# Windowed attention and gated MLP on one core: all engines' order as one explicit list, scores of a pair in one burst, norms by single tiles

## The chip, the core and the metric

The kernel runs on one core of one Trainium2 chip. The core has a matrix engine (TensorE; its matmuls are PE in the profile, its weight loads PEld), a vector engine (VectorE, DVE), an activation engine (ScalarE, ACT), a general engine (GpSimd, POOL) and a queue that issues the transfers from and to memory (SyncE, SP). Each engine works through its own list of instructions in order and waits on semaphores that the others raise. The on-chip memory SBUF holds operands; TensorE writes into PSUM, from where VectorE and ScalarE read.

The metric is the device time of one execution in microseconds (us). The profile adds where that time goes. Its span runs from the first to the last instruction and is a little shorter than the device time.

## What is computed

Eight batches, eight heads, 576 positions, head size 64. Attention looks back over a window of 128 positions, with a bias that falls linearly with the distance. Its output x (576 x 512 per batch) goes through a gated MLP with a spatial mixing matrix and is added to the result.

```python
scores = scale * np.matmul(q, k.transpose(0, 1, 3, 2))
bias = slopes[:, None, None] * (-np.abs(rel).astype(np.float32))[None, :, :]
mask = (rel >= 0) & (rel < window)
scores = np.where(mask, scores + bias[None], -1000000000.0)
attn = np.exp(scores - np.max(scores, axis=-1, keepdims=True))
attn = attn / (np.sum(attn, axis=-1, keepdims=True) + 1e-09)
x = np.matmul(attn, v)                       # heads side by side: (B, S, 512)
h = gelu_tanh(x @ w_in)                      # 512 -> 1024
u, v = h[..., :512], h[..., 512:]
v_n = (v - mean(v)) / np.sqrt(var(v) + 1e-06) * g_ln
v_s = np.einsum('ts,bsd->btd', w_sg, v_n) + b_sg[None, :, None]
out = x + (u * v_s) @ w_out
```

## The kernel before

The attention is worked off in 32 *pairs* (two heads of one batch; pair n belongs to batch n // 4), the MLP in 8 *blocks*, one per batch, each after the four pairs of its batch. Everything is fp32; MLP products are made from a high and a low part of each operand (hi·hi, hi·lo, lo·hi), so an MLP product is three matmuls, all written as one source line each (L466 to L468, L489 to L491, L551 to L553).

A pair's steps (class `Pair`; the letters are the names that order tables use) are:

- q, L: loads of q/k and of v (SP).
- a, c (`scores`, L320): scores of the first and of the second half of the queries, 64 x 64 corners of the array, four at work at once; they go into tiles of the PSUM pool ps_s.
- A, C (`minima`, L260): on VectorE, the bias is added, the sign turned, and each row's minimum kept in stats. n (`copy_minima`) copies the minima into nb.
- E or e, f (`exps`, L363): exponentials with row sums on ScalarE.
- R (inverse, VectorE), r, s, S (scaling by GpSimd, L378).
- t, T, z (transposes on TensorE into the PSUM pool ps_a, L388 and L401), X, Y (`masked`, VectorE: two mask products per head into px), P (ScalarE copy).
- v (`values`, L421 and L418): px times v on TensorE into ps_a; x (`gather`, ScalarE) into xf.
- h, l, k (`high`, `low`, `low_tail`): xf is cut into a high and a low part, xs. h and k run on ScalarE for the first five pairs and as casts on VectorE for the rest (L260); l runs on GpSimd (L438).

A block (`mlp_block`) has the parts v (sums L489 to L491, then gelu and `norm` per 128 rows), t (`v_tail`, the last 64 rows, L517, L519, and their norm into vA and vB), u (four sums L466 to L468 with a gelu over all), y (four gating sums with ws, L551 to L555, a product on VectorE, and its high and low part) and o (four output sums, the addition of x, and the transfer out). The gating sums need all norms: their twelve first matmuls read vn, the last two vA and vB. `norm` takes statistics on VectorE, a power on GpSimd, the centring on VectorE, the high part on ScalarE (L479) and the low part on VectorE (L482). A v part does gelu over two 512-wide tiles at once into one buffer vg.

Weights come as 64-bit values; twelve chunks of them are decoded (`split64`) by two ScalarE steps, three VectorE steps (L235, L237, L239), and three more on GpSimd and ScalarE.

What sets the order: the first five pairs, the decoding of w_in and some v sums of batch 0 stand in a table START, whose steps are chained on each engine. Afterwards a loop emits pair stages and block parts by small tables (PLAN), the decoding of w_sg and w_out rides along with one step for every second VectorE instruction (class `Vec`), and the tile framework's own scheduler places the instructions on the engines by its reckoning of time. TensorE's order can thus break a run of scores with a matmul of a block.

Of the kernel before, what the change touches and what calls it, by code (L numbers as in the profile page):

```python
# [21 lines left out]
def attention_gmlp(  # L22
# [116 lines left out]

    NS = 2 * (T + 1)  # L140
# [18 lines left out]
    def stage(src, cast=F32):  # L159

        w = mlp.tile([P, src.shape[1]], src.dtype, name="wst", tag="g", bufs=NF)
        nc.sync.dma_start(w[0:src.shape[0]], src)
        return w

    def w_chunk(k):

        half, c = 1 - k // NC, k % NC
        hs = slice(half * F, (half + 1) * F)
        return w_in[c * P:(c + 1) * P, hs], lambda w: split64(wi[:, 0, c, hs], wi[:, 1, c, hs], w, scratch[:, k, :])

    def chunks():

        for c in range(T):
            yield w_sgT[c * P:(c + 1) * P, :], lambda w, c=c: split_sg(c, w)
        yield w_sgT[T * P:S, :], split_sg_tail
        for c in range(NF):
            yield w_out[c * P:(c + 1) * P, :], lambda w, c=c: grouped(split64(wo[:, 0, c, :], wo[:, 1, c, :], w, att.tile([P, F], F32, name="tmp", tag="e", bufs=4)), (3, 1, 2, 1))

    def grouped(steps, sizes):
        for n in sizes:  # L180
            for _ in range(n):
                next(steps, None)
            yield

    def decode():

        jobs = chunks()
        staged = []
        def ahead(n):
            while len(staged) < n:  # L190
                job = next(jobs, None)
                if job is None:
                    return
                staged.append((stage(job[0]), job[1]))
        ahead(NEARLY)
        while staged:
            w, steps = staged.pop(0)
            yield from steps(w)
            ahead(NEARLY)

    def split_sg(c, st):
        split(ws[:, 0, c, :], ws[:, 1, c, :], st)
        yield

    def split_sg_tail(st):
        nc.sync.dma_start(st[R:2 * R], w_sgT[T * P:S, :])
        nc.scalar.activation(wsA, st, AF.Copy)
        nc.gpsimd.tensor_tensor(wsB[0:R], st[0:R], wsA[0:R].bitcast(F32), ALU.subtract)
        yield

        sb = mlp.tile([P, S], F32, name="wst", tag="g", bufs=NF)
        sh = mlp.tile([P, S], F32R, name="wsh", tag="g", bufs=NF)
        sel = const.tile([P, 1], F32, name="bsel")
        nc.vector.memset(sel[R:R + 2], -1.0)
        nc.vector.memset(sel[R:R + 1], 0.0)
        for r in range(2):
            nc.sync.dma_start(sb[R + r:R + r + 1, :], b_sg.rearrange("(o t) -> o t", o=1))
        nc.scalar.activation(sh[R:R + 2], sb[R:R + 2], AF.Copy)
        nc.vector.scalar_tensor_tensor(out=wsB[R:R + 2], in0=sh[R:R + 2].bitcast(F32), scalar=sel[R:R + 2], in1=sb[R:R + 2], op0=ALU.mult, op1=ALU.add)
        nc.vector.memset(vB[R:R + 2].bitcast(F32), 1.0)  # L220
        yield
# [26 lines left out]

    def split(hi, lo, x):
        nc.scalar.activation(hi, x, AF.Copy)  # L250
        nc.gpsimd.tensor_tensor(lo, x, hi.bitcast(F32), ALU.subtract)  # L251

    class Vec:

        credit = 0.0
        done = 0

        def __getattr__(self, name):
            def call(*args, **kw):
                inst = getattr(nc.vector, name)(*args, **kw)  # L260
                if self.steps is not None:
                    self.credit += RATE
                    while self.credit >= 1.0:
                        self.credit -= 1.0
                        self.done += 1
                        with tc.issue_after(inst.ins):
                            next(self.steps, None)
                return inst
            return call

    vec = Vec()
    vec.steps = None
# [12 lines left out]
    class Pair:  # L285
# [25 lines left out]
        def scores(self, t2):  # L311
            qk, heads = self.qk, self.heads
            W = 3 * R
            if t2 == 0:
                self.pr = [att.tile([P, T, P], F32, name="e", bufs=4) for _ in range(2)]
                self.e0 = att.tile([R, 2 * R], F32, name="e0", bufs=2)
            banks = self.banks[t2] = [ps_s.tile([P, 512], F32, name="ps_s") for _ in range(2)]
# [17 lines left out]
            burst(insts)  # L335

        def shift(self, h, dst, src, bs, acc):

            vec.tensor_tensor_reduce(out=dst, in0=src, in1=bs, scale=-1.0 / math.sqrt(D), scalar=3e38, op0=ALU.add, op1=ALU.min, accum_out=acc)

        def minima(self, t2):
            W = 3 * R
            banks, pr, nm = self.banks.pop(t2), self.pr, self.nm
            for j in range(2):
                h = 2 * self.hp + j
                sv = banks[j][:, 0:2 * W].rearrange("p (t b c) -> p t b c", t=2, b=3)
# [7 lines left out]
        def copy_minima(self):  # L354

            nb = att.tile([P, NS], F32, name="nb", bufs=3)
            vec.tensor_copy(nb, self.nm)
            self.nm = nb
# [325 lines left out]
```

## Time and profile before

| what | us |
|---|---|
| device time, median of 3 runs | 675.34 |
| lowest, highest | 674.81, 679.94 |
| the profiled execution's own time | 675.89 |
| its span | 674.2 |
| PE busy / DVE / ACT / POOL | 638.0 / 417.2 / 334.1 / 244.2 |

Mean granted TensorE clock 0.983. Rows of the profile name the line, engine and operation, then output tile <- input tiles with their shapes, then a count; in timeline rows the first two numbers are start and length in us, and the bracket at the end tells how long the engine stood idle before it and what ended that. A score or a value matmul leaves two records; MLP matmuls and transposes leave one. A matmul's row is as long as the matmul takes from entering to leaving the array, and the next one starts before it ends: what TensorE can do per us is read from start to start. A run, here, is an unbroken sequence of TensorE records of one kind.

### The profile page before, as it was taken

The numbers are of one execution on the slowest core, as the hardware profiler recorded it, in microseconds if no ns is written. First come the engines' busy times: TensorE is split into PE (matmuls) and PEld (weight loads), VectorE is DVE, ScalarE is ACT, GpSimd is POOL, SyncE is SP. The second block draws the span as 40 slices with busy tenths as digits, with TensorE's granted clock in tenths as the row PEclk, the third lists the DMA queues.
The fourth block names the chain that finished last, engine by engine and source line by source line (L and its number), as shares of the span: only waits on it lengthen the run. The fifth ranks groups of instructions, "written<-read, shape, count | busy, mean of one in ns | idle before, by whom it ended". The sixth has DMA issues, their size and how long they took to land.

```text
span 674.2 us, 14921 instructions
## 1 busy us (share of the span) xinstructions
PE 638.0 (95%) x5664; PEld 562.6 (83%) x5664; DVE 417.2 (62%) x1372; ACT 334.1 (50%) x979; POOL 244.2 (36%) x241
## 2 busy tenths in 40 slices
PE   3788796999999999999999999999999999999997
PEld 2666585887898889888899889889799888999997
DVE  5887996556646665655576656646576657553511
ACT  7676776434574326633645336742645345731420
POOL 1786657332134322551324321453226321360120
PEclk9998797999999999999999999999999999999999
DMA  8648330233212312224122322133221331001001
GB/s 273 209 128 241 114 125 8 74 106 111 72 48 80 112 53 73 73 74 143 57 59 69 107 73 73 41 103 116 69 59 56 108 106 36 1 2 71 0 1 71
DMA packets 55931, 57.24 MB, mean 85 GB/s; under 512 B 8498, under 2 KB 45362, under 8 KB 55860
## 3 DMA queue, kind: packets, MB, share of 16 engines
q1 hardware_dynamic: 55860, 56.28, 26.7%
q8 instruction: 45, 0.74, 0.5%
q14 instruction: 26, 0.21, 0.1%
HBM read 46.83 MB, written 9.44 MB: 83 GB/s over the span
## 4 chain that ended last, share of the span: by engine, by line
PE 75%; DVE 13%; ACT 7%; DMA 2%; issue 2%; POOL 1%; ACTq 0%; DVEq 0%; POOLq 0%
PE ps_m L466 9%; PE ps_m L467 8%; PE ps_m L468 8%; PE ps_s L320 7%; PE ps_a L418 7%; PE ps_m L551 5%; PE ps_m L552 5%; PE ps_m L553 5%; PE ps_a L388 4%; PE ps_m L489 3%; PE ps_m L490 3%; PE ps_m L491 3%; ACT e L363 3%; DVE vn L482 2%; DVE px L260 2%; DVE st L474 2%
## 5 line engine op out<-in xcount | busy, mean ns | idle before, releaser
L378 POOL TENSOR_TENSOR e<-e,rr 128x512 f32<-128x512 f32 (+1 forms) x96 | 77.9, 833 | 170.7 <-DVE rr L260 140.9
L363 ACT ACTIVATE e<-e,nb 128x128 f32<-128x128 f32 x270 | 101.7, 378 | 28.8 <-DVE nb L260 28.7
L320 PE MATMUL ps_s<-qk 64*64 64x192 f32 (+2 forms) x1280 | 79.7, 326 | 12.3 <-DMA qk<-qkT 8.0
L466 PE MATMUL ps_m<-xs,wi 128*128 128x288 f32 x256 | 79.2, 309 | 0.9 <-ACT vg L509 0.5
L551 PE MATMUL ps_m<-ws,vn 128*128 128x288 f32 x256 | 79.1, 309 | 0.0
L466 PE MATMUL ps_m<-g,wo 128*128 128x288 f32 x256 | 77.9, 305 | 0.2 <-DVE xf L564 0.2
L477 POOL TENSOR_TENSOR rs<-rs,mhalf 128x1 f32<-128x1 f32 (+1 forms) x40 | 35.3, 893 | 116.2 <-DVE rs L476 116.2
L552 PE MATMUL ps_m<-ws,vn 128*128 128x288 f32 x256 | 77.1, 301 | 0.0
L468 PE MATMUL ps_m<-xs,wi 128*128 128x288 f32 x256 | 76.9, 300 | 0.0
L553 PE MATMUL ps_m<-ws,vn 128*128 128x288 f32 x256 | 76.8, 300 | 0.0
L467 PE MATMUL ps_m<-g,wo 128*128 128x288 f32 x256 | 76.7, 301 | 0.0
L467 PE MATMUL ps_m<-xs,wi 128*128 128x288 f32 x256 | 76.6, 299 | 0.0
L320 PEld LDWEIGHTS ps_s<-qk 64*64 64x64 f32 x1280 | 50.2, 141 | 31.0 <-issue 18.9
L468 PE MATMUL ps_m<-g,wo 128*128 128x288 f32 x256 | 75.7, 297 | 0.0
L251 POOL TENSOR_TENSOR g<-u,g 128x576 fp32r<-128x576 f32 x32 | 45.4, 1419 | 68.3 <-ACT g L250 62.8
L418 PE MATMUL ps_a<-px,vt 128*64 128x128 f32 (+1 forms) x1152 | 64.4, 267 | 4.6 <-issue 2.8
L418 PEld LDWEIGHTS ps_a<-px,vt 128*64 128x64 f32 x1152 | 59.3, 142 | 10.3 <-issue 8.9
L260 DVE CUSTOM_DVE_ANT_0 e<-ps_s,bias 128x128 f32<-128x128 f32 (+1 forms) x256 | 57.1, 265 | 0.4
L260 DVE TENSOR_TENSOR px<-ps_a,m_old 128x512 f32<-128x512 f32 x64 | 43.8, 685 | 19.8 <-PE ps_a L388 19.5
L489 PE MATMUL ps_m<-wi,xs 128*128 128x512 f32 x128 | 52.5, 410 | 2.4 <-ACT xs L433 2.4
L438 POOL TENSOR_TENSOR xs<-xf,xs 128x576 fp32r<-128x576 f32 x32 | 46.4, 1461 | 21.1 <-DVE xs L260 20.9
L551 PEld LDWEIGHTS ps_m<-ws,vn 128*128 128x128 f32 x256 | 49.2, 192 | 3.7 <-issue 2.2
(113 smaller groups left out, 1487.6 us busy)
## 6 DMA issues: line engine op xcount, KB each, us to landing
qk<-qkT SPq DMA_DIRECT2D x32, 576.0 KB, 3.9
vt<-v_in SPq DMA_DIRECT2D x64, 256.0 KB, 3.2
outT<-xf SPq DMA_DIRECT2D x32, 288.0 KB, 2.1
wst<-w_in SPq DMA_DIRECT2D x8, 512.0 KB, 7.2
vt<-v_in SPq DMA_DIRECT2D x64, 32.0 KB, 2.9
wst<-w_out SPq DMA_DIRECT2D x4, 512.0 KB, 3.9
wst<-w_sgT SPq DMA_DIRECT2D x4, 288.0 KB, 4.1
vd<-v_in SPq DMA_DIRECT2D x64, 16.0 KB, 2.1
```

The lines of the kernel that those rows point to most:

```text
L260: inst = getattr(nc.vector, name)(*args, **kw)
L320: return lambda: nc.tensor.matmul(dst, qk[js, 0, q0:q0 + R], qk[js, 1, k0:k1], start=True, stop=True)
L363: nc.scalar.activation(x, x, AF.Exp, bias=self.nm[0:n, i:i + 1], scale=-1.0, accum_out=self.sm[0:n, i:i + 1])
L378: nc.gpsimd.tensor_tensor(x, x, self.rr[0:n, i:i + m].rearrange("p (m o) -> p m o", o=1).broadcast_to([n, m, c]), ALU.mult)
L418: return lambda: nc.tensor.matmul(x1[heads[j], q0 + lo // 2 * R if t < 0 else q0 + t * R:q0 + (hi + 1) // 2 * R], block, px[j][:, (half * ...
L466: nc.tensor.matmul(dst, ah, bh, start=(i == 0), stop=False)
L467: nc.tensor.matmul(dst, ah, bl, start=False, stop=False)
L468: nc.tensor.matmul(dst, al, bh, start=False, stop=(i == n - 1))
L489: nc.tensor.matmul(pv[:, i, :], xh, wi[:, 0, c, F:], start=(c == 0), stop=False)
L551: nc.tensor.matmul(y, vn[:, 0, t, fs], ws[:, 0, t, ss], start=(t == 0), stop=False)
L552: nc.tensor.matmul(y, vn[:, 0, t, fs], ws[:, 1, t, ss], start=False, stop=False)
L553: nc.tensor.matmul(y, vn[:, 1, t, fs], ws[:, 0, t, ss], start=False, stop=False)
```

## The change

Every engine's order for the whole program now comes from one table ORDER of about 1900 step names, which a class `Planner` runs one by one; each instruction is chained behind the one before it on its engine, as START did for the first part. Each step has a declared engine, length and needs; at build time the lengths do nothing (the list is already made from them), and the needs are only asserted. START, PLAN, `Vec` and the decode generator go. With the order, some steps change:

- From the sixth pair on a pair's scores are one step (`*`), 20 matmuls in a row; its first half goes into two tiles of ps_a, its second into two of ps_s, and its values (3, V) go into ps_s. Before, all scores went to ps_s and all values to ps_a. The first five pairs keep separate halves.
- Minima and exponentials are single steps per head and half (A, B, C, G; e, E, f, F; j for the first 64 positions); the exponentials read the minima in stats directly, so nb and its copy go.
- e0 becomes a 128-row tile, zeroed once at the start, and its transpose is 128 x 128 instead of 64 x 128.
- h and k run on ScalarE for all pairs.
- The first value product (x2) is its own step, apart from the 18 others.
- Gelu and norm of the v part work on single 512-wide tiles, vg having two buffers; the tail uses two vg tiles.
- A block's parts stand in another order (batch 0: v, v, tail, then u), and the sum of the output part c = 0 is cut so that its last quarter is a step of its own.

```diff
-        def scores(self, t2):
+        def scores(self, *t2s):
+            insts = [x for t2 in t2s for x in self.score_list(t2, ps_a if len(t2s) > 1 and t2 == 0 else ps_s)]
+            burst(insts)
+
+        def score_list(self, t2, pool):
...
-            banks = self.banks[t2] = [ps_s.tile([P, 512], F32, name="ps_s") for _ in range(2)]
+            banks = self.banks[t2] = [pool.tile([P, 512], F32, name=pool.name) for _ in range(2)]
...
-        def copy_minima(self):
-
-            nb = att.tile([P, NS], F32, name="nb", bufs=3)
-            vec.tensor_copy(nb, self.nm)
-            self.nm = nb
...
-            nc.tensor.transpose(self.ct0[:, 0:R], self.e0, ident[0:R, 0:R])
+            nc.tensor.transpose(self.ct0[:, 0:P], self.e0, ident)
...
-            if self.n < XS_ACT:
-                nc.scalar.copy(hi_of(xs), self.xf)
-            else:
-                vec.tensor_copy(hi_of(xs), self.xf)
+            nc.scalar.copy(hi_of(xs), self.xf)
...
+        def run(self, order):
+            done, taken = set(), {c: [] for c in self.bufs}
+            assert sorted(order) == sorted(self.steps)
+            for n in order:
+                _, _, _, run, after, _, take, _, _ = self.steps[n]
+                assert done.issuperset(after), n
...
+                yield run
+                done.add(n)
...
+            put("*", "PE", 1.9, [f"q{n}", ("z", n - 2)], take=es + [("ps_a", [f"A{n}"]), ("ps_a", [f"B{n}"]), ("ps_s", [f"C{n}"]), ("ps_s", [f"G{n}"])])
...
+        add(f"m{k}", "DVE", 0.38, at, go, [f"d{k}"], port=True)
+        add(f"b{k}", "DVE", 0.38, at, go, [f"m{k}"], port=True)
+        add(f"o{k}", "DVE", 0.64, at, go, [f"b{k}"], port=True)
...
-            nc.scalar.activation(vg, pv, AF.Gelu_apprx_tanh)
...
+                st[f"v{t}"] = mlp.tile([P, F], F32, name="vg", bufs=2)
+                nc.scalar.activation(st[f"v{t}"], st[f"pv{t // 2 * 2}"][:, t % 2, :], AF.Gelu_apprx_tanh)
...
-    IN_ORDER = [('t', 0), ('v', 2), ('v', 0), ('u', 0), ('u', 1), ('u', 2), ('u', 3)]
-    FIRST_ORDER = [('v', 0), ('v', 2), ('u', 0), ('u', 1), ('u', 2), ('t', 0), ('u', 3)]
...
+    IN_ORDER = [('t', 0), ('u', 0), ('v', 2), ('u', 1), ('v', 0), ('u', 2), ('u', 3)]
+    FIRST_ORDER = [('v', 0), ('v', 2), ('t', 0), ('u', 0), ('u', 1), ('u', 2), ('u', 3)]
...
+    ORDER = """
+        i0 i11 i2 d0 q0 m0 d11 b0 o0 i7 d2 m11 +0 q1 a0 m2 H0 b11 -0 A0 L0 d7 o11 B0 +11 i3 e0 c0 m7 b7 H11 C0 q2 E0 -11
...
+    """
     last = {}
-    wchunks = {}
...
+    for run in plan.run(ORDER.split()):
         before = len(nc.cur_bb.bb.instructions)
-        start_step(token[0], int(token[1:]))
+        run()
```

What the list makes of the engines' queues, at the places that matter below. On TensorE before, in the middle of the program, between output sums of a block (L466 to L468), the first half of a pair's scores:

```order
1226 L468 MATMUL ps_m<-g,wo 128x288
1227 L320 MATMUL ps_s<-qk 64x64
1228 L320 MATMUL ps_s<-qk 64x128
1229 L320 MATMUL ps_s<-qk 64x64
1230 L320 MATMUL ps_s<-qk 64x128
1231 L320 MATMUL ps_s<-qk 64x192 x5
1232 L466 MATMUL ps_m<-g,wo 128x288
1233 L320 MATMUL ps_s<-qk 64x192
1234 L320 MATMUL ps_s<-qk 64x64 x2
1235 L466 MATMUL ps_m<-g,wo 128x288
```

One output matmul stands within the half, and the second half follows elsewhere. TensorE now, between gating sums (L558, L703, L704):

```order
1515 L704 MATMUL ps_m<-wsB,vB 128x288
1516 L247 MATMUL ps_a<-qk 64x64
1517 L247 MATMUL ps_a<-qk 64x128
1518 L247 MATMUL ps_a<-qk 64x64
1519 L247 MATMUL ps_a<-qk 64x128
1520 L247 MATMUL ps_a<-qk 64x192 x6
1521 L247 MATMUL ps_a<-qk 64x64 x2
1522 L247 MATMUL ps_s<-qk 64x192 x8
1523 L556 MATMUL ps_m<-ws,vn 128x288
```

Both halves, 20 matmuls, now stand together. Over the whole program the scores of TensorE's queue stand in 86 runs before and in 34 now.

On VectorE, ahead of the first block's tail norm (vA), on which the first gating sums wait; L235 and L239 decode weights, the casts are h and k of a pair. Before:

```order
266 L239 SCALAR_TENSOR_TENSOR tmp<-wst,tmp 128x512
267 L475 BN_AGGR mv<-st 64x2
268 L260 COPY nb<-stats_131 128x10
269 L476 TENSOR_SCALAR rs<-mv 64x1
270 L478 SCALAR_TENSOR_TENSOR vg<-vg,mv,gb 64x512
271 L260 CAST xs<-xf 128x576
272 L260 COPY_PREDICATED ps_s<-sel,ps_s 128x2x64 x2
273 L260 CAST xs<-xs 128x64
274 L260 TENSOR_SCALAR rr<-stats_131 128x10
275 L260 RECIPROCAL rr<-rr 128x10
276 L235 TENSOR_SCALAR tmp<-tmp 128x512
277 L482 SCALAR_TENSOR_TENSOR vA<-vg,rs,vA 64x512
```

Now:

```order
279 L576 BN_STATS st<-vg 64x6
280 L577 BN_AGGR mv<-st 64x2
281 L578 TENSOR_SCALAR rs<-mv 64x1
282 L584 SCALAR_TENSOR_TENSOR vg<-vg,mv,gb 64x512
283 L318 TENSOR_TENSOR px<-ps_a,m_old 128x4x2x64
284 L318 TENSOR_TENSOR px<-ps_a,m_own 128x4x2x64
285 L592 SCALAR_TENSOR_TENSOR vA<-vg,rs,vA 64x512
```

The casts and the decoding of weights are gone from here; mask products of a pair stand between the centring and vA instead. The number of VectorE steps ahead of vA is nearly the same.

On SP, the first transfers before:

```order
1 L298 DMA qk<-qkT 128x1152
2 L637 DMA gb<-g_ln 128x512
3 L162 DMA wst<-w_in 128x512 x3
4 L298 DMA qk<-qkT 128x1152
5 L306 DMA vt<-v_in 128x4x128
```

and now:

```order
1 L168 DMA wst<-w_in 128x512
2 L168 DMA wst<-w_out 128x512
3 L168 DMA wst<-w_in 128x512
4 L221 DMA qk<-qkT 128x1152
5 L168 DMA wst<-w_in 128x512
```

The first pair's q/k load moved from the first place behind three weight loads.

## What is predicted

> **What bounds the kernel now.** I read the page first, then busy time by stretches, then TensorE's timeline, then the chain at the start. The page's first rows:
>
> ```profile
> span 674.2 us, 14921 instructions
> PE 638.0 (95%) x5664; PEld 562.6 (83%) x5664; DVE 417.2 (62%) x1372; ACT 334.1 (50%) x979; POOL 244.2 (36%) x241
> ```
>
> TensorE is the bound, but 95% hides two things: a matmul row overlaps the next one, so busy time is not work, and the granted clock dips early only (next rows). Busy time by stretches (columns: stretch, its length, PE, PEld, DVE, ACT, POOL with instruction counts, clock, DMA share, GB/s):
>
> ```profile
> 0.00:20.00 20.00, 8.61 (x80) 5.66 (x80) 11.37 (x60) 14.37 (x50) 4.41 (x15) 1.00 0.83 265
> 20.00:100.00 80.00, 67.41 (x629) 54.14 (x627) 69.69 (x211) 55.87 (x167) 55.28 (x49) 0.91 0.51 160
> 100.00:108.30 8.30, 4.57 (x45) 4.05 (x45) 7.10 (x18) 7.61 (x28) 6.44 (x6) 1.00 0.19 49
> 160.00:640.00 480.00, 478.55 (x4265) 426.96 (x4264) 292.50 (x958) 227.66 (x654) 154.20 (x152) 1.00 0.23 70
> ```
>
> From 160 to 640 TensorE idles 1.45 us of 480; there a change pays only by making TensorE's own work shorter. Up to 108 us VectorE is the busy one (69.69 of 80 us in the second row), and TensorE waits for it. So the sum has two terms: when the gating matmuls (y) of batch 0 can run, and what TensorE needs from there to the end.
>
> **Term 1, the first y.** TensorE's rows around it:
>
> ```profile
> 104.27 0.29 PE L553 MATMUL ps_m<-ws,vn 128*128 128x288 f32 x1
> 111.09 0.61 PE L554 MATMUL ps_m<-wsA,vA 128*128 128x288 f32 x1 [6.53 <-DVE vA L482]
> 114.62 0.44 PE L554 MATMUL ps_m<-wsA,vA 128*128 128x288 f32 x1
> 114.86 0.44 PE L555 MATMUL ps_m<-wsB,vB 66*128 66x288 f32 x1
> ```
>
> TensorE stands 6.53 us for the last tail norm (vA) and then runs at half pace for a while: 0.24 us from start to start at 114.62, against 0.13 later. So real gating starts at 111.1. The same VectorE work stands ahead of vA in both orders (four mask products more, two casts and two copies less, which about cancels). VectorE was busy 11.37 + 69.69 + 7.10 = 88.2 us by 108.3, and idle 20.1. Two parts of this can shrink. The first is stretch, in the three VectorE steps that decode weights:
>
> ```profile
> L235 DVE TENSOR_SCALAR tmp<-tmp x12: 365/424/5109, 10.6 to 107.9; 128x512 f32<-128x512 f32 x12
> L237 DVE TENSOR_SCALAR tmp<-tmp x12: 366/426/2498, 11.0 to 111.1; 128x512 int32<-128x512 int32 x12
> L239 DVE SCALAR_TENSOR_TENSOR tmp<-wst,tmp x12: 679/686/2771, 14.4 to 112.0; 128x512 int32<-128x512 int32 x12
> ```
>
> (min/median/max in ns.) The three longest alone lose 4.7 + 2.1 + 2.1 = 8.8 us over their medians. The new list places these steps by lengths of 0.38, 0.38 and 0.64, and keeps them off GpSimd's steps in its own reckoning; real times drift from it, so I take half: 4.4. The second is idleness: 20 - 11.37 = 8.6 us of it lie in the first 20 us, and stay, because the first q/k load now stands behind three weight loads while the first weights come earlier. Of the other 11.5 I take half, 5.8, since weights, pairs and norms now interleave by length and not by one decode step per two VectorE steps. First y: 111.1 - 4.4 - 5.8 = 101 us. Bounds: 111 (nothing gained) and 91 (all of both).
>
> The Trainium skill, "SBUF — State Buffer", section "Who interferes with whom", speaks against the 4.4: VectorE in a two-port mode or with two SBUF inputs and GpSimd share a port pair as an exclusive lock, and the loser is blocked for the other's whole instruction. The 5109 ns row agrees in direction, and looks like more than one such instruction in a row. By that rule a list that drifts keeps its full stretch: first y at 105.4, and the time 4.4 us more than the sum below.
>
> **Term 2, TensorE's work from the first y on.** It is priced by starts in the timeline. Blocks first (from the timeline and from the chain):
>
> ```profile
> 616.02 1.09 PE L517 MATMUL ps_m<-wi,xs 128*128 128x512 f32 x4
> 641.87 0.30 PE L551 MATMUL ps_m<-ws,vn 128*128 128x288 f32 x1
> 642.00 0.29 PE L552 MATMUL ps_m<-ws,vn 128*128 128x288 f32 x1
> 670.23 0.76 DVE L564 TENSOR_TENSOR xf<-ps_m,xf 128x576 f32<-128x576 f32 x1 [2.44 <-PE ps_m L468]
> 317.80 1.13 PE ps_m L517 x4
> 472.22 1.13 PE ps_m L517 x4
> ```
>
> The last MLP block runs alone from 616.0 to 670.2: 54.2 us, of which y and output from 641.9 are 28.3. Two blocks with their eight pairs take 472.22 - 317.80 = 154.4, so one block and four pairs take 77.2, and a pair costs (77.2 - 54.2) / 4 = 5.75 us of TensorE. Where those go:
>
> ```profile
> 299.63 0.89 PE L320 MATMUL ps_s<-qk 64*64 64x64 f32 x18
> 300.45 0.40 PE L466 MATMUL ps_m<-g,wo 128*128 128x288 f32 x1
> 300.78 0.54 PE L320 MATMUL ps_s<-qk 64*64 64x192 f32 x6
> 301.24 0.40 PE L466 MATMUL ps_m<-g,wo 128*128 128x288 f32 x1
> 301.48 0.29 PE L467 MATMUL ps_m<-g,wo 128*128 128x288 f32 x1
> 304.42 0.27 PE L401 MATMUL ps_a<-ident,e 64*128 64x64 f32 x1
> 304.62 0.88 PE L320 MATMUL ps_s<-qk 64*64 64x192 f32 x16
> 306.88 0.60 PE L388 MATMUL ps_a<-ident,e 128*128 128x128 f32 x4
> 307.31 0.33 PE L421 MATMUL ps_a<-p,vd 128*128 128x64 f32 x2
> 307.57 1.00 PE L320 MATMUL ps_s<-qk 64*64 64x64 f32 x24
> 308.50 0.40 PE L466 MATMUL ps_m<-g,wo 128*128 128x288 f32 x1
> 308.74 0.29 PE L467 MATMUL ps_m<-g,wo 128*128 128x288 f32 x1
> 311.89 1.88 PE L418 MATMUL ps_a<-px,vt 128*64 128x64 f32 x36
> 313.70 0.40 PE L466 MATMUL ps_m<-g,wo 128*128 128x288 f32 x1
> 313.94 0.29 PE L467 MATMUL ps_m<-g,wo 128*128 128x288 f32 x1
> ```
>
> An MLP matmul is 0.13 from start to start (641.87 to 642.00), but 0.24 right behind scores or values (308.50 to 308.74), and going into scores costs 0.33 - 0.13 = 0.20 (300.45 to 300.78). An uncut run of 24 score records takes 308.74 - 307.57 - 0.13 = 1.04 us net. The same 24 cut into 18 and 6 by one MLP matmul take 301.48 - 299.63 - 0.26 = 1.59. So one cut costs 0.55 us; its bare edges, 0.20 in and 0.11 out, are 0.31, the lower bound. The scores of 20 pairs between 165 and 551 us, by their source line:
>
> ```profile
> L320 PE MATMUL ps_s<-qk x800: 216/322/373, 180.1 to 547.8; 64*64 64x192 f32 x131, 64*64 64x64 f32 x24, 64*64 64x128 f32 x5
> ```
>
> In the timeline these 800 records stand in 54 runs, 2.7 a pair; the new order has one a pair from the sixth pair on. That saves 1.7 x 0.31 = 0.53 to 1.7 x 0.55 = 0.94. The first transpose, now 128 wide, goes from 0.20 (304.42 to 304.62) to a quarter of the 0.43 of four (306.88 to 307.31): 0.09. I take 0.85 in all, nearer the whole measured cut than its bare edges: a pair costs 4.9 us (4.7 to 5.15).
>
> Behind the first y stand 28.3 (y and output of batch 0), seven blocks 7 x 54.2 = 379.4, the 24 whole pairs 8 to 31 at 4.9 = 117.6, and what the new order leaves of pairs 6 and 7: two values at 313.94 - 311.89 - 0.13 = 1.92 with their 0.26 (307.31 to 307.57), and nine transposes, 0.97; 5.3. Sum 530.6.
>
> **The small edits.** xs casts go from VectorE to ScalarE:
>
> ```profile
> L260 DVE CAST xs<-xf 128x576 fp32r<-128x576 f32 x27 | 30.3, 1139 | 23.1 <-PE ps_m L468 13.7 <-ACT xf L426 9.4
> L433 ACT CAST xs<-xf 128x576 fp32r<-128x576 f32 x5 | 3.3, 666 | 0.0
> ```
>
> The two engines stand at 62% and 50%, so 27 x 0.67 = 18 us more on ScalarE lie beside TensorE's work; if that cover went, a late cast would hold a whole block's first matmuls. The dropped copy of the minima, gelu and norm by single 512 tiles (smaller ScalarE steps, more of them) and two memsets at the start cost nothing under the same cover; ACT table loads are 32 before and 30 after.
>
> New waits: scores now take both ps_a tiles, so a step on ps_a right behind a burst waits for VectorE's first minima, some 1.0 us at a place. I found one such place (transposes of pair 15 behind the scores of pair 16); I take 4 us for it and its like, between 0 and one per pair, 24.
>
> **Sum.** 101 + 530.6 + the end behind the last matmul, 674.2 - 670.2 = 4.0, + 4 = 639.6 of span. The profiled execution took 675.89 for its 674.2, so 1.7 goes on top: 641 us, against that execution's 675.89 and the median of 675.34. About 1% (6.8 us) is what a measurement of this kernel tells from no change.
>
> **Rivals.** *The start gives nothing.* VectorE stays as stretched and idle as before, the first y comes at 111.1, and half pace (4.7 us of it, costing about 2.1) comes again: 641 + 10 + 2 = 653. For it: equal VectorE work. Against: 20 us of idleness and 8.8 of stretch are there to win. The Trainium skill, "TensorE: Matmul & The Clock Gate", section "HAM oscillation — how this bites in real kernels", has idle gaps over about 3.4 us bring the half clock back; the 6.53 us gap and the 0.24 pace behind it agree, so a shorter wait would spare both. *A cut is worth only its edges, and the start gives nothing:* pair 5.15, 653 + 24 x 0.25 = 659; with a wait in every second pair about 665. *Everything gained:* first y at 91, pair 4.7, no waits: 641 - 10 - 5 - 4 = 622. *The change doesn't do what it says:* the order shows whole runs of scores, and TensorE runs its queue in order, so a wait within a run would add waiting but no cut; unlikely, and it would be a form of the next. *Slower: scores in all four tiles of ps_a and ps_s.* A burst needs both ps_a and both ps_s empty and leaves four VectorE steps to empty them. Its price:
>
> ```profile
> 6.46 0.30 DVE L260 COPY_PREDICATED ps_s<-sel,ps_s 128x128 f32<-128x128 uint8 x1 [2.33 <-PE ps_s L320]
> 7.48 0.28 DVE L260 COPY_PREDICATED ps_s<-sel,ps_s 128x128 f32<-128x128 uint8 x1
> ```
>
> One minima step with a first block is 1.02 us. If at each of 24 pairs TensorE stood for two of them and for one more before the next burst, 3.1 x 24 = 73 us would come on, 641 - 4 + 73 = 710. It decides from (675 + 7 - 637) / 24 = 1.9 us a pair. Against: halves of u and y (1.6 to 1.9 us) stand between a burst and the next step on ps_a at nearly every place.
>
> **How the numbers follow.** Forecast, 626 to 650: 0.65. Start gives nothing, alone or with small cuts, 650 to 668: 0.19. Everything gained, under 626: 0.05. PSUM waits eat the gain, within 1%: 0.06; more than that, slower: 0.05. Faster 0.89, same 0.06, slower 0.05. The range 625 to 662 leaves out slower and same, 0.11, some 0.04 above 662 and 0.04 below 625.
>
> **What would show it.** Right: the first y's vA matmul near 101 us; the distance of two blocks' tail matmuls near 2 x 73.8 = 148 and not 154; score runs of 40 records with the next MLP matmul some 1.5 to 1.8 us on; TensorE idle from 160 us on under 10 us. Wrong: vA still at 111 (term 1), block distance over 151 with TensorE busy (size of a cut), or TensorE rows that wait for DVE ps_a or e steps in every block (waits).

## The result, and the profile after

The changed kernel takes 644.86 us in the median of 4 runs (644.43 to 645.17); the kernel before, timed beside it, 675.62 (674.81 to 679.94). The ratio is 0.953, 95% interval 0.949 to 0.957. The forecast was 641 us, 625 to 662. The profile page of the changed kernel, its span, the engines' busy time, the granted clock in 40 slices and the chain that ended last:

```profile
span 643.3 us, 14843 instructions
PE 602.2 (94%) x5664; PEld 550.4 (86%) x5664; DVE 381.5 (59%) x1291; ACT 358.4 (56%) x1047; POOL 240.3 (37%) x243
PEclk9988979999999999999999999999999999999999
PE 84%; DVE 7%; POOL 3%; issue 2%; DMA 2%; ACT 1%; POOLq 0%; SPq 0%; DVEq 0%; ACTq 0%
```

TensorE is the bound as before, with 35.8 us less of busy time; the clock dips only in the first 100 us. Busy time by stretches of the changed kernel (columns as in the prediction), the first two of the start, the third behind the vA matmul of the first y:

```profile
20.00:86.00 66.00, 46.63 (x505) 35.37 (x501) 61.05 (x196) 51.39 (x168) 51.71 (x47) 0.94 0.63 195
86.00:110.80 24.80, 24.39 (x212) 23.25 (x213) 19.59 (x60) 16.42 (x38) 9.49 (x10) 0.89 0.12 30
110.80:643.30 532.50, 524.80 (x4891) 487.34 (x4889) 289.36 (x988) 275.36 (x800) 171.15 (x169) 1.00 0.23 73
```

and the same last stretch of the kernel before:

```profile
111.09:674.20 563.11, 557.46 (x4914) 498.71 (x4914) 326.27 (x1084) 253.51 (x736) 175.91 (x170) 0.99 0.22 69
```

So the 30.9 us of span split cleanly: 30.6 came from behind the vA matmul (563.1 to 532.5) and 0.3 from ahead of it (111.09 to 110.80). The prediction had expected 10 of them ahead of it. Some of the 30.6 is work that changed sides: 8 transposes, one first transpose and 16 score records that stood behind the vA matmul before now stand ahead of it, some 2 us by an estimate from the starts in the traces.

Why the start gained nothing shows in the timeline of the changed kernel, three engines between 79 and 89 us (start, length, engine, line; in brackets the idle time before and what ended it):

```profile
81.77 2.39 POOL L299 TENSOR_TENSOR e<-e,rr 64x128 f32<-64x128 f32 x3 [2.72 <-ACT vn L589]
81.80 3.57 DVE L592 SCALAR_TENSOR_TENSOR vn<-vg,rs,vn 128x512 fp32r<-128x512 f32 x2 [0.20 <-ACT vn L589]
82.22 0.33 PE L322 MATMUL ps_a<-ident,e 128*128 128x128 f32 x1 [2.40 <-POOL e L299]
85.30 0.28 DVE L273 COPY_PREDICATED ps_a<-sel,ps_a 128x128 f32<-128x128 uint8 x1
86.41 1.09 PE L309 MATMUL ps_a<-ident,e 128*128 128x128 f32 x4 [3.86 <-DVE stats L266]
87.53 0.44 PE L557 MATMUL ps_m<-xs,wi 128*128 128x288 f32 x1
87.77 0.44 PE L558 MATMUL ps_m<-xs,wi 128*128 128x288 f32 x1
```

TensorE finished pair 6's scores at 79.8 and then ran one transpose in 6.6 us. The transposes of pair 5 wait for a ps_a tile that pair 6's scores hold; VectorE begins to empty it only at 85.30, behind two norm steps that take 3.57 us together beside three GpSimd steps. Behind the stop TensorE runs at half pace, 0.24 us from start to start. From 86.4 us on it hardly stands (24.39 of 24.80 us busy) until the first y, whose rows in the timeline are these, with VectorE's step that makes vA ready:

```profile
107.33 0.74 DVE L592 SCALAR_TENSOR_TENSOR vA<-vg,rs,vA 64x512 fp32r<-64x512 f32 x1 [0.68 <-ACT vA L589]
109.09 0.40 PE L556 MATMUL ps_m<-ws,vn 128*128 128x288 f32 x1
110.80 0.30 PE L703 MATMUL ps_m<-wsA,vA 128*128 128x288 f32 x1
```

vA is ready at 108.07, 3 us earlier than before (111.04), and nobody waits for it: before, TensorE stood 6.53 us here; now it arrives 2.7 us after vA. VectorE's same step in the kernel before, in its timeline:

```profile
108.27 2.76 DVE L482 SCALAR_TENSOR_TENSOR vA<-vg,rs,vA 64x512 fp32r<-64x512 f32 x1
```

Behind the first y TensorE's waits come to 3.8 us in five rows (the view of waits: line, what ended them, us in total, times, longest):

```profile
PE ps_m L556 <- DVE vg L647: 1.5, 1, 1.5
PE ps_a L247 <- PE ps_a L322: 0.8, 1, 0.8
PE ps_a L309 <- POOL g L716: 0.7, 1, 0.7
...
PE ps_a L309 <- DVE stats L266: 0.3, 1, 0.3
```

A burst of scores in the timeline of the changed kernel, between two block sums:

```profile
310.60 0.39 PE L558 MATMUL ps_m<-wi,xs 128*128 128x512 f32 x1
310.92 0.94 PE L247 MATMUL ps_a<-qk 64*64 64x64 f32 x22
...
311.74 0.83 PE L247 MATMUL ps_s<-qk 64*64 64x192 f32 x14
312.50 0.40 PE L556 MATMUL ps_m<-xs,wi 128*128 128x288 f32 x1
312.74 0.30 PE L557 MATMUL ps_m<-xs,wi 128*128 128x288 f32 x1
```

The 40 records take 1.58 us from first start to the next block matmul. Counted in the timeline behind the vA matmul, the scores stand in 24 such runs, in the kernel before in 71.

### The profile page after: what moved, and what is told of

Read it like the earlier page. It is cut to its first block, busy times and chain, and to the rows that moved or that the text cites. A ratio compares the mean times of both kernels' runs of the same rounds, so it can differ in the third digit from the quotient of the medians.

```text
span 643.3 us, 14843 instructions
## 1 busy us (share of the span) xinstructions
PE 602.2 (94%) x5664; PEld 550.4 (86%) x5664; DVE 381.5 (59%) x1291; ACT 358.4 (56%) x1047; POOL 240.3 (37%) x243
## 4 chain that ended last, share of the span: by engine, by line
PE 84%; DVE 7%; POOL 3%; issue 2%; DMA 2%; ACT 1%; POOLq 0%; SPq 0%; DVEq 0%; ACTq 0%
PE ps_m L556 21%; PE ps_m L558 19%; PE ps_m L557 19%; PE ps_s L342 7%; PE ps_a L309 4%; PE ps_s L247 4%; PE ps_a L247 3%; PE ps_m L704 1%; PE ps_m L703 1%; DMA qk<-qkT 1%; DVE e L266 1%; POOL e L299 1%; DVE px L318 1%; DVE vn L592 1%; PE ps_m L640 1%
## 5 line engine op out<-in xcount | busy, mean ns | idle before, releaser
L282 ACT ACTIVATE e<-e,stats 128x128 f32<-128x128 f32 (+1 forms) x320 | 121.2, 380 | 27.6 <-DVE stats L266 26.0
L556 PE MATMUL ps_m<-ws,vn 128*128 128x288 f32 x256 | 78.5, 307 | 0.0
L558 PE MATMUL ps_m<-xs,wi 128*128 128x288 f32 x256 | 76.3, 298 | 0.0
L558 PE MATMUL ps_m<-g,wo 128*128 128x288 f32 x256 | 75.9, 296 | 0.0
L557 PE MATMUL ps_m<-ws,vn 128*128 128x288 f32 x256 | 75.6, 295 | 0.0
L558 PE MATMUL ps_m<-ws,vn 128*128 128x288 f32 x256 | 75.6, 295 | 0.0
L581 POOL TENSOR_TENSOR rs<-rs,mhalf 128x1 f32<-128x1 f32 (+1 forms) x40 | 32.1, 804 | 103.7 <-DVE rs L578 103.7
L282 ACT ACTIVATION_READ_ACCUMULATOR e<-e,stats 128x1 f32 (+1 forms) x320 | 60.1, 188 | 0.0
L739 DVE TENSOR_TENSOR xf<-ps_m,xf 128x576 f32<-128x576 f32 x32 | 24.2, 757 | 58.9 <-PE ps_m L558 58.7
L247 PE MATMUL ps_s<-qk 64*64 64x192 f32 (+2 forms) x632 | 42.1, 362 | 15.8 <-DMA qk<-qkT 10.9
L709 DVE TENSOR_TENSOR u<-ps_m,u 128x576 f32<-128x576 f32 x32 | 24.3, 758 | 51.5 <-PE ps_m L704 48.5
L556 PEld LDWEIGHTS ps_m<-xs,wi 128*128 128x128 f32 x256 | 49.1, 192 | 4.4 <-issue 2.5
L309 PE MATMUL ps_a<-ident,e 128*128 128x128 f32 x256 | 40.7, 286 | 11.3 <-DVE stats L266 4.2
```

The source lines that it names most:

```text
L247: return lambda: nc.tensor.matmul(dst, qk[js, 0, q0:q0 + R], qk[js, 1, k0:k1], start=True, stop=True)
L282: nc.scalar.activation(x, x, AF.Exp, bias=self.nm[0:n, i:i + 1], scale=-1.0, accum_out=self.sm[0:n, i:i + 1])
L309: burst([lambda t=t: nc.tensor.transpose(ct[:, t * P:(t + 1) * P], self.pr[j][:, t, :], ident) for t in range(T)])
L556: nc.tensor.matmul(dst, ah, bh, start=(first and i == 0), stop=False)
L557: nc.tensor.matmul(dst, ah, bl, start=False, stop=False)
L558: nc.tensor.matmul(dst, al, bh, start=False, stop=(last and i == n - 1))
```

## The experiments

Two questions are open. What were the 30.6 us behind the first y, which is 6 more than predicted? And what holds the start? All kernels below are the changed kernel with one edit, or, in the last three rows of the table, with several edits added up. Two numbers are read from each: the median time, and, from the trace, the start of the first vA matmul and the rest of the span behind it. Between executions whose lists are the same up to there, that matmul falls anywhere from 110.0 to 112.9 us, while the rest repeats to 0.1 us. So prices of TensorE's work are read from the rest, and a gain of the start under about 2 us is not told from chance by one trace. The rows come from several chips, on which the kernel before took 675.6 to 677.4 us in the median; the control ran on the chip of "no add" and of "u, B6 and P5 early".

| kernel | median us (lowest to highest) | ratio to before, 95% | vA matmul | rest |
|---|---|---|---|---|
| changed kernel | 644.86 (644.43–645.17) | 0.953, 0.949–0.957 | 110.8 | 532.5 |
| the same again (control) | 644.76 (644.05–645.35) | 0.951, 0.948–0.954 | 110.4 | 532.5 |
| one cut | 653.88 (653.51–656.44) | 0.966, 0.962–0.970 | 112.6 | 542.1 |
| two cuts | 663.94 (662.97–665.25) | 0.980, 0.975–0.984 | 112.9 | 550.7 |
| z 64 wide | 650.65 (649.56–651.89) | 0.961, 0.957–0.965 | 110.4 | 538.3 |
| casts on VectorE | 644.38 (643.85–645.45) | 0.952, 0.947–0.956 | 110.0 | 532.5 |
| q0 first | 646.38 (645.01–648.22) | 0.954, 0.951–0.958 | 112.1 | 532.5 |
| no clamp | 645.34 (644.70–646.50) | 0.953, 0.948–0.958 | 111.1 | 532.5 |
| no add | 646.34 (643.57–647.42) | 0.953, 0.949–0.957 | 112.3 | 532.5 |
| u early | 643.99 (642.39–644.38) | 0.950, 0.947–0.954 | 110.2 | 532.5 |
| u early, B6 early | 642.65 (641.44–643.10) | 0.949, 0.945–0.952 | 108.2 | 532.5 |
| u, B6 and P5 early | 642.36 (642.04–643.65) | 0.948, 0.945–0.951 | 107.9 | 532.5 |
| the same, less decoding | 639.95 (639.33–642.74) | 0.947, 0.942–0.952 | 106.1 | 532.6 |

**What a cut costs.** From pair 8 on, the burst is cut behind its first half; the second half follows three matmuls of the next block sum later (one cut), or in two pieces (two cuts). C and the steps behind it keep their order.

```diff
         def scores(self, *t2s):
...
-            burst(insts)
+            if self.n < NPAIR * 2:
+                burst(insts)
+                return
+            burst(insts[:12])
+            pending.append(insts[12:])
...
             nc.tensor.matmul(dst, al, bh, start=False, stop=(last and i == n - 1))
+            if pending:
+                burst(pending.pop(0))
```

For two cuts the line reads `pending.extend([insts[12:16], insts[16:]])`.

> From pair 8 on each burst of scores is cut once: behind its first 24 records come three matmuls of the next MLP step, then its last 16. That is 24 cuts behind the first y; the first 100 us and the orders of the other engines stay. Theory A, a cut costs what the kernel before showed in one place, 0.55 us: 13 us more, 658. Theory B, a cut costs only its bare edges, 0.31 us: 7.4 us more, 652. Theory C, the gain came from something else than whole bursts (casts, fewer waits): under 3 us more. The minima behind the cut come 0.5 to 0.8 us later, which should lie beside TensorE's work.

> As the kernel with one cut, but with the last 16 records cut once more into 8 and 8, with three MLP matmuls between: 48 cuts, 2 a pair, near the 2.7 runs a pair of the kernel before. Theory A: 26 us more than 645, 671. Theory B: 15 us more, 660. Theory C: under 5 us more. If the price is per cut, the second cut costs as much as the first; if the first costs more, it is the delay of the minima and not the cut.

The rest grows by 9.6 us for 24 cuts and by 18.2 for 48: 0.40 a cut for the first, 0.36 for the second, 0.38 in the mean. That lies between the prices of theories A (0.55) and B (0.31), nearer the bare edges. Theory C falls: whole bursts are a large part of the gain. The timeline of the kernel with one cut shows where it goes (its line numbers stand 6 higher):

```profile
215.24 0.29 PE L564 MATMUL ps_m<-g,wo 128*128 128x288 f32 x1
215.46 1.00 PE L253 MATMUL ps_a<-qk 64*64 64x64 f32 x24
216.39 0.40 PE L562 MATMUL ps_m<-xs,wi 128*128 128x288 f32 x1
216.63 0.30 PE L563 MATMUL ps_m<-xs,wi 128*128 128x288 f32 x1
216.76 0.29 PE L564 MATMUL ps_m<-xs,wi 128*128 128x288 f32 x1
216.98 0.88 PE L253 MATMUL ps_s<-qk 64*64 64x192 f32 x16
217.79 0.40 PE L562 MATMUL ps_m<-xs,wi 128*128 128x288 f32 x1
```

The pieces take 0.93 and 0.81, 1.74 together against 1.58 uncut: 0.16. Going in again takes 0.22 in place of 0.13 (216.76 to 216.98), going out 0.24 in place of 0.13 (216.39 to 216.63): 0.09 and 0.11. Sum 0.36.

**What the 64-wide transpose costs.** From pair 8 on, z is as before:

```diff
-            nc.tensor.transpose(self.ct0[:, 0:P], self.e0, ident)
+            if self.n < 8:
+                nc.tensor.transpose(self.ct0[:, 0:P], self.e0, ident)
+            else:
+                nc.tensor.transpose(self.ct0[:, 0:R], self.e0[0:R], ident[0:R, 0:R])
```

> From pair 8 on the first transpose of a pair (z) is 64 wide again, from 64 rows, as in the kernel before; 24 of them, order unchanged. Theory A, it costs its own length, 0.20 against 0.09 us as the prediction had it: 24 times 0.11, 2.6 us more than 645, so 647 to 648. Theory B, a 64-wide transpose is another tiling of TensorE's array, as scores are, so the row behind it pays for going back: in the kernel before z's start to start was 0.20 and that of the transpose ahead of it 0.20 where others have 0.03 to 0.11; then it is 0.25 to 0.27 each, 6 to 6.5 us, 651. Theory C, hidden: within 1 us of 645.

The rest grows by 5.8 us, 0.24 for each of 24, and the median lies 5.9 above the control's. This is theory B. In the timeline of this kernel a z stands among gating sums:

```profile
195.33 0.29 PE L707 MATMUL ps_m<-wsB,vB 66*128 66x288 f32 x1
195.55 0.27 PE L325 MATMUL ps_a<-ident,e 64*128 64x64 f32 x1
195.75 0.41 PE L559 MATMUL ps_m<-ws,vn 128*128 128x288 f32 x1
196.00 0.29 PE L560 MATMUL ps_m<-ws,vn 128*128 128x288 f32 x1
```

and in the changed kernel, among u and v sums (a 512-wide matmul takes 0.23):

```profile
300.59 0.40 PE L558 MATMUL ps_m<-wi,xs 128*128 128x512 f32 x1
300.83 0.28 PE L322 MATMUL ps_a<-ident,e 128*128 128x128 f32 x1
300.86 0.38 PE L556 MATMUL ps_m<-xs,wi 128*128 128x288 f32 x1
301.07 0.30 PE L557 MATMUL ps_m<-xs,wi 128*128 128x288 f32 x1
```

The wide one adds 0.03 for itself and 0.08 to the matmul behind it. The narrow one adds 0.09 to the matmul ahead, 0.20 for itself and 0.12 to the one behind, 0.30 more than the wide one at these two places; the mean of all 24 is 0.24. Its row shows another tiling of the array (64*128, ahead of the tile's shape, against 128*128), and its edges are like those of the scores, 0.09 in and 0.11 out; so the reading is that it pays for going into that tiling and back. A narrow transpose without a change of tiling was not run. The Trainium skill, "TensorEngine Tiling (Array Packing)", section "Tiling Modes", has a change of tiling mode drain TensorE, without a price; the trace agrees in that both edges cost time, and these are the prices.

**The casts.** From pair 8 on, h and k run as `nc.vector.tensor_copy` again, at the same places of the list.

> From pair 8 on the two casts of a pair's output (576 wide and 64 wide) are on VectorE again, as in the kernel before, at the same places of the list; 24 pairs times 0.67 and 0.23 us go from ScalarE to VectorE. Theory A (the prediction's): both engines have room beside TensorE's work, the time stays within 2 us of 645, and TensorE's waits behind the first y stay under 6 us (3.9 now). Theory B, the move of the casts is part of the gain because VectorE's steps hold PSUM tiles: waits of TensorE for VectorE's minima and mask products come on, 0.3 to 0.6 us a pair, 652 to 660.

Theory A holds: the rest does not move. From 110 to 640 us of the changed kernel, and then of this one, VectorE is busy 20.7 us more and ScalarE 20.4 less, and TensorE notices neither:

```profile
110.00:640.00 530.00, 525.61 (x4897) 488.14 (x4895) 289.94 (x995) 276.16 (x800) 171.95 (x169) 1.00 0.23 73
```

```profile
110.00:640.00 530.00, 524.80 (x4891) 487.26 (x4889) 310.62 (x1036) 255.72 (x752) 171.32 (x169) 1.00 0.23 72
```

**The late first load.** `q0` goes to the front of the list, ahead of i0, i11 and i2.

> The load of the first q and k, which stands behind three weight loads in SyncE's queue, is moved ahead of them; nothing else moves. In the changed kernel TensorE's first scores start at 10.86 us (4.67 before) and VectorE has little to do until then. Theory A, the late start is carried through to the first y: scores start about 6 us earlier, the vA matmul of the first y comes at 105 to 107 us instead of 110.80, and the time falls from 645 to 639 to 642. Theory B, the start is decided later, by VectorE's and GpSimd's weight steps between 70 and 86 us and by what stands behind them on TensorE: the vA matmul stays at 110 to 112 us and the time within 1.5 us of 645.

Theory B holds, with vA at 112.1 us and no gain in time. The first scores start 6.2 us earlier, and the second half of pair 0 waits (timeline of this kernel):

```profile
4.63 1.76 PE L247 MATMUL ps_s<-qk 64*64 64x64 f32 x24 [4.63 <-DMA qk<-qkT]
14.63 0.87 PE L247 MATMUL ps_s<-qk 64*64 64x192 f32 x2 [8.23 <-DVE stats L266]
```

VectorE's list has pair 0's minima behind the first weight steps, and those now come later, since the weights are loaded later. The earlier load alone gained nothing here, since the list sets the place of the step that uses its result.

**Less work for VectorE, for GpSimd.** The first of the three VectorE steps of the decoding is left out (no clamp), or GpSimd's addition in it (no add).

```diff
-        nc.vector.tensor_scalar(f, f, TINY64, None, ALU.max)
```

```diff
-        nc.gpsimd.tensor_tensor(fi, fi, ri, ALU.add)
```

> Leaves out the clamp of tiny weights, the first of three VectorE steps in the decoding of each of the 12 weight tiles (12 steps, 6.2 us busy, 2 to 3 of it drawn out beyond their median). Theory A, VectorE's total work sets the first y: the vA matmul comes 4 to 6 us earlier than 110.80 and the time falls to 639 to 641. Theory B, waits between engines at single places of the list set it (TensorE stands from 82.55 to 86.41 for one minima step that is behind two long steps): 0 to 3 us, 642 to 645.

> Leaves out the step of GpSimd that adds the low bits in the decoding of each of the 12 weight tiles (12 steps of 1.3 us; the weights then lack their lowest bits). GpSimd stands almost nowhere between 19 and 66 us (32.87 of 40 us busy from 20 to 60). Theory A, GpSimd sets the start, by its own work and by drawing out VectorE's steps beside it: eleven steps lie ahead of 86 us, 14 us less, and the vA matmul comes 6 to 14 us earlier, at 97 to 105; the time is 631 to 640. Theory B, no one engine sets it, the chain goes from engine to engine at the places that the list fixed: at most 3 us, as with the 5 us that VectorE lost without gain. Theory C, waits for loads and for TensorE take its place: 3 to 6 us.

There is no gain either time, as theory B allowed, also for GpSimd, which is busy 51.7 of the 66 us from 20 to 86 in the changed kernel. The same stretch, no clamp first, then no add:

```profile
20.00:86.00 66.00, 47.56 (x505) 37.16 (x501) 56.73 (x185) 50.04 (x166) 51.50 (x47) 0.93 0.63 194
```

```profile
20.00:86.00 66.00, 49.35 (x506) 38.74 (x501) 54.76 (x192) 49.09 (x164) 39.44 (x38) 0.92 0.60 189
```

Without the additions GpSimd loses 12.3 of its 51.7 us in this stretch, and VectorE beside it 6.3 of 61.05 with 192 instructions in place of 196, so most of that was steps drawn out. The first y still comes at 112.3 us. Neither engine's total alone sets the start, busy as they are.

**Single steps at the place of the stop.** On TensorE both halves of the first u block go ahead of the first transpose of pair 5 (u early); on VectorE the second minima of pair 6 go ahead of two norm steps (B6); on ScalarE the copy of pair 5's first transpose goes ahead of two gelu steps (P5). The lists of the three engines in step names (u000 and u001 are the halves of the first u sum of batch 0, vn00 and vg02 steps of its v part):

```diff
 TensorE
-*6 z5 t5 u000 T5 u010 u001 u011
+*6 u000 u001 z5 t5 T5 u010 u011
 VectorE
-R5 vn00 vn01 B6 C6
+R5 B6 vn00 vn01 C6
 ScalarE
-e6 vg03 vg02 d8 P5
+e6 P5 vg03 vg02 d8
```

> On TensorE the two halves of the first u block (3.2 us of work, its last input is a weight step of GpSimd that ends at 79.05 us) are put ahead of the first transpose of pair 5, behind which TensorE stood from 79.82 to 82.22 and from 82.55 to 86.41 us and then ran some 9 us at a lower pace (matmuls 0.27 apart). Theory A, TensorE's own queue from 86.4 us on sets the first y: 3.2 us of work go into idle time and the low pace is mostly spared; the vA matmul comes at 106 to 107.6 us instead of 110.80 and the time falls by 3 to 5 us, to 640 to 642. Theory B, the tail norm on VectorE sets it (vA was ready at 108.07): the matmul cannot come before 108, the gain is at most 2.7 us, and a wait for vA appears ahead of it.

> As the kernel with the first u block put earlier on TensorE, and on VectorE the second minima step of pair 6, which empties the PSUM tile that the transposes of pair 5 wait for, goes ahead of two steps of the norm (3.57 us together, drawn out beside GpSimd). Theory A, that one wait holds the start: the transposes of pair 5 come at 83 to 84 us instead of 86.4 to 88.6, nothing runs at a low pace from there, the vA matmul comes at 106 to 107.5 us and the time is 640 to 641.5. Theory B, VectorE's work only changes places: the norm steps come 1.2 us later, with them the gelu and the second u block, TensorE waits there instead, and the gain over the u block alone (643.99 measured) is under 1 us.

> As the kernel with the first u block and the minima of pair 6 put earlier, and on ScalarE the copy of pair 5's first transpose goes ahead of two gelu steps that wait for the norm on VectorE. There TensorE still stood 3.4 us, to 87.36, and ran at a lower pace behind it (matmuls 0.24 apart until 92.6). Theory A, single waits at this place hold the start: the second four transposes of pair 5 come at 84.5 to 85.5, the stop behind them is under 2.5 us, the low pace is gone, the vA matmul comes at 105.5 to 107 instead of 108.24, and the time is 640 to 641.5. Theory B, the second u block still cannot start before the gelu at 86 us empties its tile: TensorE stands as long, only one place further, the low pace stays, and the time is within 1 us of 642.65.

> The changed kernel itself, beside the others on the same chip: 645 us (644.4 to 645.2 measured), vA matmul at 110 to 113 us.

The kernel with u early alone is inconclusive: 0.8 us by the medians, and its trace had pair 6's scores end 2.2 us later than in the changed kernel, so that the vA matmul came only 0.6 earlier. With B6 the transposes come at 83.4 instead of 86.4, and the stop moves behind them. The vA matmul at 108.2 us and the gain of 1.3 us over u early lie between what theories A and B said (timeline of that kernel):

```profile
83.38 0.60 PE L309 MATMUL ps_a<-ident,e 128*128 128x128 f32 x4
87.36 1.09 PE L309 MATMUL ps_a<-ident,e 128*128 128x128 f32 x4 [3.38 <-issue]
88.48 0.44 PE L557 MATMUL ps_m<-xs,wi 128*128 128x288 f32 x1
```

With P5 as well that stop is 1.2 us, and the next one comes at the values of pair 5 (timeline of that kernel; 36 value records take 1.88 us at full clock):

```profile
85.80 0.40 PE L555 MATMUL ps_m<-xs,wi 128*128 128x288 f32 x1 [1.20 <-ACT vg L629]
...
91.48 0.35 PE L342 MATMUL ps_s<-px,vt 128*64 128x64 f32 x4 [2.07 <-DVE px L318]
92.08 3.20 PE L342 MATMUL ps_s<-px,vt 128*64 128x128 f32 x32 [0.25 <-DVE px L318]
```

So P5 went as theory B had it: the stop wandered on, and the third edit brought 0.3 us by the medians, which is not told from nothing. The three together beat the changed kernel: 642.36 against 644.76 of the control on the same chip, and no run of the one (642.04 to 643.65) is as slow as the fastest of the other (644.05). The gain is 0.4%.

**Both together.** In that kernel, clamp and addition are both left out.

> The kernel with the three steps moved at 80 to 88 us (vA matmul 107.9, 642.36 us), and from the decoding of the 12 weight tiles both VectorE's clamp and GpSimd's addition of the low bits are left out (about 5 and 14 us of work ahead of 86 us). Theory A, each engine alone hid behind the other: together they free the start, the vA matmul comes at 95 to 104 and the time is 631 to 638. Theory B, what sets the start is the order of steps with their hops from engine to engine, and TensorE's own work at its place in that order: the vA matmul stays at 106 to 111 and the time at 641 to 646, though VectorE and GpSimd are idle 19 us more.

The vA matmul comes at 106.1 us, in theory B's range; the median of 639.95 lies between the two theories' ranges. From 20 to 86 us VectorE is busy 5.8 and GpSimd 11.4 us less than in the kernel with the three steps moved, some 17 us together. For that the vA matmul comes 1.8 us earlier and the median is 2.4 lower, on another chip, with one of four runs (642.74) among those of the other kernel. So the work of the two engines together may have a small part in the start; what the run does not show is a gain of the size that theory A named.

## Why the prediction came out where it did

The time is within the range and 3.9 us over the forecast, but two terms were off in opposite directions: in the profiled execution the first y came 9.8 us later than the sum had it, and the rest of the span was 6.1 us shorter. That the two nearly cancel is luck.

**Term 1, the first y at 101.** This is the step that failed: "First y: 111.1 - 4.4 - 5.8 = 101 us". It took the time that VectorE might save as time by which the first y comes earlier. Neither saving came in its size. The three decode steps fell by 2.9 us, from 29.2 to 26.3 us busy, but all of VectorE's work up to the vA matmul takes 92.2 us with 304 instructions, where it took 90.9 with 289; its idle time there fell by 1.6 us, from 20.2 to 18.6. What got better is the tail norm: from its sums on TensorE to vA it now takes 10 us (98.1 to 108.07) and took 18 before (93.0 to 111.04). But TensorE comes to the tail's sums 5 us later than before, and to the vA matmul 2.7 us after vA is ready; that TensorE itself would be late was not among the prediction's cases. The experiments say more: 5 us less of VectorE's work, 12 us less of GpSimd's and a first load 6 us earlier each alone brought no gain, and the one gain that is clear of the noise, 2.4 us, came from single steps moved at one stop; with these in place, less work on both engines may have brought some 2 us more. These runs fit a start that is a chain from engine to engine in the order of the list, shortened where TensorE stands. What sets the time up to 78 us stays open: the load and either lightened engine alone do not, and no step was moved there.

The sentence on the Trainium skill's port lock ("SBUF — State Buffer", "Who interferes with whom") described the trace: two vn steps of 3.57 us beside three GpSimd steps, and 6.3 us less on VectorE when GpSimd's additions went. The price that it was to have, 4.4 us, cannot be told, since the stretch alone was not what held the first y.

**Term 2, TensorE's work of 530.6.** The method held: work priced from start to start in the old trace. Measured from the vA matmul to the last matmul it is 528.6, of which 3.8 are waits, so 524.8, and 5.8 too much was forecast. The largest mis-sized part is the first transpose, whose saving was taken from its own length alone, some 0.1 a pair; the run gives 0.24, and with 24 to 26 of them the difference is 3 us. Another 1.6 us was counted twice: the 28.3 for y and output begins with the first gating matmul of the last block (641.87), but the sum sets it behind the vA matmul, and twelve gating matmuls, 0.13 apart, stand ahead of that one. The cuts came out nearly right by luck, two errors that cancel: 0.38 each and not some 0.44, but 47 fewer runs and not 41, about 18 us either way. What is left, about 1 us, has no run of its own; values stand in 41 runs instead of 50, which at 0.2 for going in and out is 1.8, worked out and not tested. In the change as a whole (30.6 behind the first y), about 18 are the cuts at the price that the runs gave, some 6 the transposes, some 2 the half pace behind the old wait for vA, which is gone, and some 2 the work that now stands ahead of the vA matmul; the remaining 2 to 3 us have no run.

**Small edits at nothing.** Right for the casts, which were tried; the dropped copy, the single-tile norms and the memsets were not tried one by one, and TensorE waits for VectorE's vg step once behind the first y, 1.5 us.

**New waits of 4 us.** Right in sum, 3.8, but largely by luck: only two of the five waits, 1.0 us, stand at transposes, where the forecast had looked for them. At those of pair 15 behind the scores of pair 16, forecast at 1.0, 0.7 is in the trace; the profile puts that down to a GpSimd step, and VectorE's first minima of pair 16 end within 0.2 us of the wait's end too, so which of the two held it is not shown. The slower rival, a wait at every pair for the four PSUM tiles, did not come.

**The rivals.** "The start gives nothing", at 653 with a chance of 0.19, is what happened to the start; its time was 8 us too long, 2 because half pace came back at another place, ahead of the first y and not behind it, and 6 by the error in term 2.

**What was to show it.** Blocks: from the tail sums at 160.5 to those at 531.7 five blocks take 74.2 us each, where 73.8 was forecast; the same five took 78.0 before. Bursts: 1.58 us, within 1.5 to 1.8. Idle time from 160 us on: under 4 us, within 10. Only vA near 101 did not come; vA still at 111 was the prediction's own sign that term 1 was wrong.

## What to carry to other kernels

Price a small matmul by what it does to its neighbours: where it ran in another tiling of the array than the work around it, going in and out cost about as much as the transpose itself here (0.21 and 0.20 us), so put such matmuls together, or pad them to the common shape. Busy time saved on an engine is not time saved unless something waits for that engine last; at a start like this one, where four engines are 71 to 92% busy, look for the place where the bounding engine stands, see which one step ends that wait, and move that step. Here each such move uncovered the next stop, so take the gain of a move from a run and not from the length of the stop.

## What the runs showed that was not expected

- The span behind the first vA matmul is 532.5 or 532.6 us in ten traces, though that matmul falls between 106.1 and 112.3: whatever the start did, and with 20 us of casts moved between two engines, TensorE's time behind it stayed the same.
- A 64-wide transpose from 64 rows costs 0.24 us more than a 128-wide one from 128 rows, half of whose input is zeros.
- TensorE fell to half pace behind a stop of 2.07 us: the granted clock of the last kernel but one ("u, B6 and P5 early"), eighth column, in two stretches of 2 us:

```profile
90.00:92.00 2.00, 0.35 (x4) 0.20 (x4) 2.00 (x6) 1.94 (x6) 0.00 (x0) 0.92 0.00 0
92.00:94.00 2.00, 1.92 (x18) 1.92 (x20) 2.00 (x5) 2.00 (x7) 0.00 (x0) 0.50 0.00 0
```

The Trainium skill, "TensorE: Matmul & The Clock Gate", section "HAM oscillation — how this bites in real kernels", warns of gaps over about 3.4 us. The stop of 3.86 us above agrees and that of 3.38 us is about at the mark; this one was shorter, and half pace followed it too.
